# An attention, gating and feed-forward kernel: every engine's instruction order written out, and two more blocks by Strassen's scheme

## Chip, cores and metric

The kernel runs on one core of one Trainium2 chip. The metric is the device time of one execution in microseconds (us). Before the change it is 735.42 us, the median of 3 runs (735.09 to 735.94).

## What is computed

Three layers follow each other, over 4 sequences of 768 tokens with 512 channels. Every input is float32.

```python
# 1. attention in chunks of 32 queries: 8 memory keys, 16 keys to the left, the chunk, 8 to the right
scores = scale * np.matmul(q_c, k_full.transpose(0, 1, 3, 2))
scores = scores - np.max(scores, axis=-1, keepdims=True)
a = np.exp(scores)
a = a / (np.sum(a, axis=-1, keepdims=True) + 1e-09)
out[:, :, c_start:c_end] = np.matmul(a, v_full)
# 2. mixing: a causal convolution of 5 taps makes a gate, which multiplies a projection
gate_pre += conv_w[k][None, None, :] * xp[:, k:k + S, :]
gate = 1.0 / (1.0 + np.exp(-gate_pre))
x = (gate * (x @ w_val)) @ w_out
# 3. normalization and feed-forward with 2048 hidden channels
xn = (x - mu) / np.sqrt(var + 1e-06) * g_ln
out = x + np.maximum(xn @ w_ch1, 0.0) @ w_ch2
```

## The kernel before

The 24 subblocks of 128 tokens are grouped into 13 blocks: block 0 has one subblock, blocks 1 to 11 have two (256 tokens), block 12 has one. Each block passes through attention (`attention32` for the first blocks, `attention` for the others), mixing (`mix`) and feed-forward (`ffn`). Float32 numbers are split into two half-precision parts, high and low, and a product is three matmuls (high by high, high by low, low by high: `PASSES`); only block 0 and parts of the next two use float32 matmuls. The high part is written by ScalarE (ACT), the low part by VectorE (DVE), so nearly every operand takes one instruction on each.

Feed-forward. `ch1` (matmuls at line 716) makes one PSUM tile `c_ps` from 24 matmuls of 256 columns, 8 tiles to a block. In a plain block, ACT takes the ReLU of it (728), DVE makes the low part (730), and `ch2` multiplies it by the second weight (756) in groups of 12 matmuls of 512 columns, eight groups to a block. In a fast block (`FAST = 5`: blocks 5 to 11) the second product goes by Strassen's scheme. Its seven products need sums of the hidden tiles, which `pair` makes four times per block (ACT at 635, 639, 645; DVE at 640 to 644 and 646), and sums of quarters of the second weight. `products` then issues 168 matmuls (line 682), nearly all of 256 columns, where `ch2` issues 96 of 512, and `fast_finish` adds the seven accumulators together (691 to 699).

The sums of quarters of the second weight are made once, by `sums_of_weights`: for each of eight row groups three steps, on DVE (604, 606, 609 to 612, 616) and ACT (615). All of it goes through the one tile `ft`, which plain blocks named in `GATES` use for the first hidden tile, and which `pair` and `fast_finish` use too. `BUILD` says how many of the 24 steps are issued within a block's feed-forward: six each in blocks 1 to 4.

Mixing. `mix` makes the gate from five taps (497 on ACT, 501 on DVE), the projection `val` (519), the output `yps` (537), the mean and variance (544 to 561, a row of small DVE instructions) and the normalized rows `xh` (562 or 564). These are split (ACT 581, DVE 582) and transposed into `xn` by DMA (issued by SP, line 584), and `ch1` of the same block reads `xn`. For blocks below `NPET = 2` the transpose is a float32 matmul with an identity instead (569), and 572 and 573 split its result.

Attention. `totals` (a matmul with ones, line 166) gives the sums of squares by which q, k and v are scaled (`pow2`, 153 to 157); then DVE writes the low parts of q (`bd`, 425) and k (`ks`, 428), and `scores` (280) needs both.

What sets the order. Attention, mixing, feed-forward, weights and loads are generators that a string of steps calls in turn (`PLAN` for the start, then `STEADY` or `FASTY` once per block); attention runs two blocks and mixing one block ahead of feed-forward. The framework's scheduler then arranges the instructions of each engine by priority, and each engine works through its own list strictly in that order.

Of the kernel before, what the change touches and what calls it, by code (L numbers as in the profile page):

```python
# [1 line left out]

# [10 lines left out]
U16 = mybir.dt.uint16  # L13
# [5 lines left out]
P = 128  # L19
# [13 lines left out]
NEVAC = 8  # L33
NXH = 4
NP = 2
FAST = 5
GATES = {1: (0,), 2: (0,), 3: (0,), 4: (0,)}
BUILD = {1: 6, 2: 6, 3: 6, 4: 6}
LAG = 1
NF32 = 2  # L40
NA32 = 3
FIRST = 1
CUT = 384
FILLS = (32, 64, 8, 16)
# [12 lines left out]

def passes(a, b):
# [6 lines left out]
def chunk_attention_moe_kernel(ctx: ExitStack, tc: tile.TileContext,  # L65
                               q, k, v, w_val, conv_w, w_out, g_ln, w_ch1, w_ch2, out):
    nc = tc.nc
    B, S, DM = out.shape
    NSUB, HP = q.shape[1], q.shape[3]
    KEYS = k.shape[5]  # L70
    DFF = w_ch1.shape[1]
    KW = conv_w.shape[1]
# [29 lines left out]
    g_sb = const.tile([P, KC], F32, name="g_sb")  # L102
# [155 lines left out]
    sub = {}  # L258
    tail = [None]

    def load(n):
        while len(sub) < min(n + 1, sum(n for _, n in blocks)):
            b, i = divmod(len(sub), NSUB)
            st = sub[len(sub)] = {}
            st["q"] = ld.tile([P, HP, SUB], F32, tag="q", name="qt")
            nc.sync.dma_start(out=st["q"], in_=q[b, i])
            st["k"] = ld.tile([P, HP, 2, KEYS], F32, tag="k", name="kt")
            nc.sync.dma_start(out=st["k"], in_=k[b, i])
            st["v"] = ld.tile([P, 2, DM], F32, tag="v", name="vt")
            if b + i > 0:  # L270
                nc.sync.dma_start(out=st["v"], in_=v[b, i])
# [117 lines left out]
        yield  # L389

    def attention(n, d, u):


        b, i = divmod(n, NSUB)
# [15 lines left out]
        s = sc_p.tile([P, 3], F32, tag="s", name="s")  # L410
# [74 lines left out]
        return d  # L485

    def mix(j):
        d = blk[j]
        T = d["T"]
        n = T // SUB  # L490
# [155 lines left out]
        nc.vector.tensor_tensor(out=o[1][1], in0=ft, in1=o[0][1], op=ALU.subtract)  # L646

    def products(d, p, u2):
        if not fast[0]:
            fast[0] = True  # L650
            nc.gpsimd.memset(W2.half(3, 0)[:, 768:1024], 0.0)
        if "acc" not in d:
            d["acc"] = [ps_a.tile([P, 2, 256], F32, tag=f"acc{u}", name=f"acc{u}") for u in range(4)]
        acc = d["acc"]
        o = d["h", p]
        half = NM // 2
        own = lambda m, c: W2.rows(m, True, c * 256, 256)
# [28 lines left out]
    def fast_finish(j):
        d = blk[j]
# [43 lines left out]
        d["h", w] = h  # L731

    def ch2(d, w):
        T = d["T"]
        c = 512 // T
        h = d.pop(("h", w))
# [57 lines left out]
    if True:  # L794
        nc.vector.memset(ones, 1.0)

        nc.scalar.activation(out=g_one, in_=ones[:, 0:1], func=AF.Exp)
        for t in (tops[0], bdt, *tops[1:], eye):
            nc.gpsimd.memset(t, 0.0)
# [13 lines left out]
        fetched = [0]
# [66 lines left out]
        def ffn(j):  # L880
# [109 lines left out]
```

## Time and profile before

| | before |
|---|---|
| median of 3 runs | 735.42 us |
| the profiled execution, its own time | 734.32 us |
| its span, first to last instruction | 732.2 us |
| TensorE (PE) busy | 709.3 us |
| VectorE (DVE) busy | 592.7 us |
| ScalarE (ACT) busy | 449.6 us |
| granted TensorE clock | 0.999 |

The profile shows one execution on the hardware. "Busy" is the time in which an engine had an instruction running; a matmul's record is longer than its pace, since matmuls are pipelined, so how fast they follow each other is read from a run of many. A wait is put down to what ended it. Stretches are given in us from the start of the span.

### The profile page before, as it was taken

Reading aid. Unit: us, or ns where it says so; the run is one execution under the profiler, and the core shown is the slowest. Engines: PE = TensorE matmul, PEld = TensorE weight load, DVE = VectorE, ACT = ScalarE, POOL = GpSimd, SP = SyncE. Lnnn points to the kernel's source line nnn. Section 1 sums busy time; section 2 is a strip of 40 time slices with the busy share of each in tenths; the row PEclk is TensorE's granted clock in tenths of the full one; section 3 lists DMA queues with packets and bytes.
Section 4 is the critical chain, followed back from the end, with each engine's and each line's share of the span. In section 5 each row is a group of like instructions: output and inputs, shape, how many; then the busy total and the mean of one; then the engine's idle time right before and its main releaser. Section 6 shows DMA issues by size and latency. Waiting matters only on the chain.

```text
span 732.2 us, 17810 instructions
## 1 busy us (share of the span) xinstructions
PE 709.3 (97%) x7501; PEld 556.1 (76%) x7501; DVE 592.7 (81%) x1297; ACT 449.6 (61%) x716; POOL 11.3 (2%) x37
## 2 busy tenths in 40 slices
PE   8889999999999999999999999999999999999998
PEld 7677776667667667668878878878878878878897
DVE  4979999979969769778789888989888888875461
ACT  4657786546556557568667677677677676652230
POOL 2000010000000000000000000000000000000000
PEclk9999999999999999999999999999999999999999
DMA  9993612141232142133033143033033012001010
GB/s 353 418 405 119 230 65 66 49 125 50 68 81 72 38 102 72 45 99 105 15 96 109 16 95 110 16 95 108 17 94 109 16 23 52 16 16 44 2 33 26
DMA packets 62271, 67.21 MB, mean 92 GB/s; under 512 B 45680, under 2 KB 45936, under 8 KB 62192
## 3 DMA queue, kind: packets, MB, share of 16 engines
q1 hardware_dynamic: 61904, 66.07, 29.0%
q8 instruction: 58, 0.95, 0.6%
q14 instruction: 21, 0.17, 0.1%
q10 hardware_dynamic: 288, 0.02, 0.0%
HBM read 49.30 MB, written 6.29 MB: 76 GB/s over the span
## 4 chain that ended last, share of the span: by engine, by line
PE 70%; DVE 16%; ACT 6%; DMA 4%; issue 2%; SPq 0%; DVEq 0%; ACTq 0%
PE c_ps L716 28%; PE acc L756 12%; PE acc L682 9%; PE yps L537 8%; PE val L519 7%; PE s_ps L280 2%; DMA xn<-xh 2%; DVE gt L501 2%; DVE bd L425 1%; PE pv L466 1%; ACT ft L635 1%; DVE ks L428 1%; PE gram L227 1%; PE pv L376 1%; DVE w L248 1%
## 5 line engine op out<-in xcount | busy, mean ns | idle before, releaser
L716 PE MATMUL c_ps<-xn,w 128*128 128x256 f16 (+1 forms) x2304 | 253.2, 268 | 4.1 <-DMA xn<-xh 4.0
L716 PEld LDWEIGHTS <-w 128*128 128x128 f16 x2304 | 216.2, 98 | 36.3 <-issue 4.6
L756 PE MATMUL acc<-w,hb 128*128 128x512 f16 (+2 forms) x448 | 103.7, 376 | 1.1 <-DVE hb L730 1.1
L501 DVE SCALAR_TENSOR_TENSOR gt<-xT,cw_sb,gt 128x256 f32<-128x256 f32 (+1 forms) x208 | 87.8, 458 | 1.7 <-ACT gt L497 1.5
L756 PEld LDWEIGHTS <-hb 128*128 128x128 f16 x432 | 41.4, 98 | 36.1 <-DVE hb L730 1.4
L682 PEld LDWEIGHTS <-hb 128*128 128x128 f16 x588 | 57.5, 98 | 8.8
L682 PEld LDWEIGHTS <-w 128*128 128x128 f16 x588 | 57.0, 98 | 6.6
L635 ACT ACTIVATE ft<-c_ps 128x512 f32<-128x512 f32 x56 | 32.5, 594 | 48.1 <-PE c_ps L716 30.4
L519 PE MATMUL val<-x,wv 128*128 128x256 f16 (+1 forms) x528 | 57.6, 268 | 0.0
L537 PE MATMUL yps<-wo,hg 128*128 128x512 f16 x252 | 56.9, 379 | 0.5 <-DVE hg L525 0.5
L519 PEld LDWEIGHTS <-wv 128*128 128x128 f16 x528 | 49.4, 98 | 6.2
L682 PE MATMUL acc<-w,hb 128*128 128x256 f16 (+1 forms) x280 | 49.6, 278 | 0.0
L326 ACT ACTIVATE xT<-pv,c_pv 64x256 f32<-64x256 f32 x70 | 32.4, 466 | 23.5 <-PE pv L466 22.8
L537 PEld LDWEIGHTS <-hg 128*128 128x128 f16 x252 | 23.8, 98 | 28.1 <-DVE hg L525 1.0
L682 PE MATMUL acc<-w 128*128 128x256 f16 x266 | 44.7, 273 | 0.0
L728 ACT ACTIVATE hb<-c_ps 128x512 f16<-128x512 f32 (+1 forms) x36 | 21.2, 588 | 34.2 <-PE c_ps L716 34.0
L682 PE MATMUL acc<-spare,hb 128*128 128x256 f16 (+1 forms) x252 | 42.0, 276 | 0.0
L682 PE MATMUL acc<-spare,w 128*128 128x256 f16 x252 | 41.2, 273 | 0.0
L730 DVE SCALAR_TENSOR_TENSOR hb<-c_ps,hb 128x512 f16<-128x512 f32 x32 | 22.0, 686 | 12.7 <-ACT hb L728 12.6
L425 DVE SCALAR_TENSOR_TENSOR bd<-qt,s,bd 64x512 f16<-64x512 f32 x38 | 28.3, 745 | 4.2 <-ACT bd L424 3.6
L640 DVE TENSOR_TENSOR hb<-ft,hb 128x768 f16<-128x768 f32 x14 | 13.4, 957 | 20.8 <-ACT hb L639 20.8
L424 ACT ACTIVATE bd<-qt,s 64x512 f16<-64x512 f32 x38 | 27.2, 716 | 3.0 <-DVE s L155 2.4
(190 smaller groups left out, 1166.0 us busy)
## 6 DMA issues: line engine op xcount, KB each, us to landing
vt<-in_v_dram SPq DMA_DIRECT2D x24, 512.0 KB, 4.3
kt<-in_k_dram SPq DMA_DIRECT2D x24, 384.0 KB, 3.7
qt<-in_q_dram SPq DMA_DIRECT2D x24, 256.0 KB, 2.6
out_dram<-y SPq DMA_DIRECT2D x23, 256.0 KB, 2.3
w<-in_w_ch_dram SPq DMA_DIRECT2D x5, 1023.5 KB, 8.8
spare<-in_w_ch_dram SPq DMA_DIRECT2D x4, 1023.8 KB, 13.7
w<-in_w_ch_dram SPq DMA_DIRECT2D x4, 1023.8 KB, 14.3
spare<-in_w_ch_dram SPq DMA_DIRECT2D x3, 1023.5 KB, 6.1
```

Of the source, the lines that this page charges most:

```text
L326: nc.scalar.activation(out=o, in_=t[pp, :, :, e, :], func=AF.Copy, scale=c_pv if isinstance(c_pv, float) else c_pv[pp])
L424: nc.scalar.activation(out=hi, in_=src, func=AF.Copy, scale=s[pp, 0:1])
L425: nc.vector.scalar_tensor_tensor(out=lo, in0=src, scalar=s[pp, 0:1], in1=hi, op0=ALU.mult, op1=ALU.subtract)
L501: nc.vector.scalar_tensor_tensor(out=o, in0=xT[:, hp, 0:n, kk:kk + SUB], scalar=cw_sb[:, kk, hp:hp + 1], in1=o, op0=ALU.mult, op1=ALU.add)
L519: nc.tensor.matmul(out=t[:, u, 0:T], lhsT=l, rhs=r, start=(x == 0), stop=(x == len(todo) - 1))
L537: nc.tensor.matmul(out=t, lhsT=l, rhs=r, start=(x == 0), stop=(x == len(todo) - 1))
L635: nc.scalar.activation(out=ft[:, at:at + 2, :].rearrange("p x (m n) -> p m x n", m=2), in_=t.rearrange("p (m x n) -> p m x n", m=2, x=2), ...
L682: nc.tensor.matmul(out=o, lhsT=l, rhs=r, start=first, stop=(p == half // 2 - 1 and u2 == 1 and end[t] == x))
L716: nc.tensor.matmul(out=t[:, u * T:(u + 1) * T], lhsT=l, rhs=r, start=(x == 0), stop=(x == len(todo) - 1))
L728: nc.scalar.activation(out=h[0], in_=t, func=AF.Relu)
L730: nc.vector.scalar_tensor_tensor(out=h[1], in0=t, scalar=0.0, in1=h[0], op0=ALU.max, op1=ALU.subtract)
L756: nc.tensor.matmul(out=a[:, 0:n], lhsT=l, rhs=r, start=(first and x == 0), stop=(end and x == len(todo) - 1))
```

## The change

Four things change together.

First, every compute engine's and SP's instructions are put in an order that is spelled out in strings. While the program is built, `mark` notes for each instruction which stream it belongs to (a and b: attention of even and odd subblocks; x and y: mixing of even and odd blocks; f: `ch1` and `pair`; g: second product and closing sums; m, p, q: weights; t: sums of weights; s, l, w: start and loads). At the end `pin` reads for each engine a string such as `x4b+7fxf2x+3`: take the next four of x, then the eighth that is left of b, then the next of f, and so on, and ties each instruction to the one named before it. The ties are for the scheduler alone: no semaphore wait is added. Second, `FAST` becomes 3: blocks 3 and 4 go by Strassen's scheme too, so nine blocks do. Third, the sums of the second weight are made in blocks 1 and 2 alone, twelve steps in each. Fourth, `NPET` becomes 1: block 1's rows are transposed by DMA like the others'. Two small loads on ACT's queue move ahead of the first instructions. The arithmetic of a block is otherwise as it was.

```diff
-FAST = 5
-GATES = {1: (0,), 2: (0,), 3: (0,), 4: (0,)}
-BUILD = {1: 6, 2: 6, 3: 6, 4: 6}
+FAST = 3
+GATES = {1: (0,), 2: (0,)}
+BUILD = {1: 12, 2: 12}
...
-NPET = 2
+NPET = 1
...
+ORDER = {
+    "PE": (
+        "s32a+16a+16a+16a+16a+16a+16a+16a+16a+16a+16a+16a69a+4a+4a+4a+4a+4a+4a+4a+4a+20a+20a+20a+20a+20a+20a+20a+20a+20a+20a+20"
...
+    "DVE": (
+        "sa4sa3samsabmm+2m+2mxx+3xx+2xx+1x3x+3xx+2x4bmxbpxmbm+2bm3bpbxaxmx2m2xbx3ax3ax3pxa4pamp2a2b+3yy+3yy+2yy+1ypy2y+3ypyy+1qyp"
...
+def runs(order):
+
+    return [(l, int(at or 0)) for l, n, at in re.findall(r"([a-z])(\d*)\+?(\d*)", order) for _ in range(int(n or 1))]
...
+    labels, label, mixing = [], ["s"], [0]
+
+    def mark(l):
+
+        labels.extend(label * (len(nc.cur_bb.bb.instructions) - len(labels)))
+        was, label[0] = label[0], l
+        return was
+
+    def pin():
+
+        seq = {e: {} for e in ORDER}
+        for i, l in zip(nc.cur_bb.bb.instructions, labels):
+            e = str(i.engine).split(".")[-1]
+            if e in seq and type(i).__name__ != "BassTilePoolBoundary":
+                seq[e].setdefault(l, []).append(i)
+        for e, todo in seq.items():
+            seq[e] = [todo[l].pop(at) for l, at in runs(ORDER[e])]
+            assert not any(todo.values())
+        follows = [z for x in seq.values() for z in zip(x, x[1:])]
+        follows.append((next(i for i in seq["Activation"][::-1] if type(i).__name__ == "InstDMACopy"), seq["SP"][0]))
+        for a, b in follows:
+            tc.add_manual_dep(b, a.name, mybir.DependencyInfo(mybir.DependencyClass.NoSync, mybir.DependencyReason.SCHED_ONLY),
+                              reason="order")
...
+        nc.scalar.dma_start(out=g_sb, in_=g_ln)
+        cw_raw = const.tile([P, KW * HP * 4], U16, name="cw_raw")
+        nc.scalar.dma_start(out=cw_raw[:, 0:KW * HP * 4 - 1],
+                            in_=conv_w.bitcast(U16).rearrange("p k c -> p (k c)")[:, 1:KW * HP * 4])
         nc.scalar.activation(out=g_one, in_=ones[:, 0:1], func=AF.Exp)
...
-        nc.scalar.dma_start(out=g_sb, in_=g_ln)
         nc.vector.tensor_tensor(out=gs_sb, in0=g_sb, in1=g_sb, op=ALU.mult)
...
-                for _ in range((i + 1) * n // len(steps) - i * n // len(steps)):
+                for _ in range(max(0, i - 1) * n // (len(steps) - 2) - max(0, i - 2) * n // (len(steps) - 2)):
                     go("t")
...
+        mark("")
+        pin()
```

The lists of DVE show what the strings move, at three places. The names: `ft` is the shared tile of sums, `w_113` and `spare` hold the second weight and its sums, `hb` and `w_113` in lines 640 to 646 (722 to 728 in the change) are the operands of the products, `xh` the normalized rows, `bd` and `ks` the low parts of q and k.

The first is DVE in block 2's feed-forward, where one row group's sums of the second weight end. Before:

```order
L611 TENSOR_TENSOR ft<-ft 128x256
L616 TENSOR_TENSOR w_112<-ft,wv 128x256
L612 TENSOR_TENSOR ft<-ft 128x256
L616 TENSOR_TENSOR spare<-ft,spare 128x768
L730 SCALAR_TENSOR_TENSOR hb<-c_ps,hb 128x512
L153 TENSOR_SCALAR e<-tot 128x3
L155 TENSOR_SCALAR s<-e 128x3
L157 TENSOR_SCALAR inv<-e 128x3
L328 TENSOR_SCALAR xT<-pv,c_pv 64x4x64 x2
L414 TENSOR_SCALAR c_exp<-inv 128x1
```

With the change (lines 686 to 698 are the old 604 to 616; 607 is 525; 375 and 376 are 306 and 307; 198 is 153; 517 is 442):

```order
L607 SCALAR_TENSOR_TENSOR hg_2228<-gt,hg_2227 128x512
L692 TENSOR_TENSOR ft<-ft 128x256
L693 TENSOR_TENSOR ft<-ft 128x256
L694 TENSOR_TENSOR ft<-ft 128x256
L698 TENSOR_TENSOR w_113<-ft,wo 128x256
L375 RECIPROCAL rs<-sum 128x8
L198 TENSOR_SCALAR e<-tot 128x3
L376 TENSOR_TENSOR sc<-sc,rs 128x512
L698 TENSOR_TENSOR spare<-ft,spare 128x768
L686 TENSOR_TENSOR ft<-w_113 128x2x256
L517 TENSOR_TENSOR p_2358<-sc,p_2357 128x512
L688 TENSOR_TENSOR ft<-w_113 128x512
```

Before, the next row group's 604 stands 58 rows behind the last 616 of this one; now its 686 follows the last 698 directly. Of the 64 DVE instructions that make the sums, 32 stood ahead of what the last `ch1` matmul of block 2 waits for, and now 57 do.

The second is DVE at the end of mixing for a block, between the last small instruction of the variance (561, now 643) and the low parts of the normalized rows (582, now 664), in the fast blocks. Before:

```order
L561 SCALAR_TENSOR_TENSOR va<-mv,rt 128x2
L640 TENSOR_TENSOR w_113<-ft,w_113 128x3x256
L641 TENSOR_TENSOR ft<-ft 128x256
L582 TENSOR_TENSOR xh_6997<-xh,xh_6996 128x512
L642 TENSOR_TENSOR ft<-ft 128x256
L643 TENSOR_TENSOR ft<-ft 128x256
L644 TENSOR_TENSOR ft<-ft 128x256
L646 TENSOR_TENSOR w_113<-ft,w_113 128x4x256
L582 TENSOR_TENSOR xh_7057<-xh,xh_7056 128x512
```

With the change:

```order
L643 SCALAR_TENSOR_TENSOR va<-mv,rt 128x2
L664 TENSOR_TENSOR xh_7203<-xh,xh_7202 128x512
L623 TENSOR_TENSOR c_y<-inv,cy_w 128x1
L722 TENSOR_TENSOR w_113<-ft,w_113 128x3x256
L723 TENSOR_TENSOR ft<-ft 128x256
L724 TENSOR_TENSOR ft<-ft 128x256
L725 TENSOR_TENSOR ft<-ft 128x256
L726 TENSOR_TENSOR ft<-ft 128x256
L664 TENSOR_TENSOR xh_7263<-xh,xh_7262 128x512
L728 TENSOR_TENSOR w_113<-ft,w_113 128x4x256
```

The low part of the first rows moves ahead of two instructions of `pair`, and that of the second rows ahead of the longest of them, 646 (now 728).

The third is DVE between the scales of a subblock (414, 417, now 489, 492) and the first use of its scores (291, now 360), in the fast blocks. Before:

```order
L417 TENSOR_SCALAR c_pv<-inv 128x1
L541 TENSOR_TENSOR c_y<-inv,cy_w 128x1
L644 TENSOR_TENSOR ft<-ft 128x256
L425 SCALAR_TENSOR_TENSOR bd<-qt,s,bd 64x16x32
L473 SCALAR_TENSOR_TENSOR x_6227<-xT,s,x_6226 128x4x128
L646 TENSOR_TENSOR hb<-ft,hb 128x1024
L425 SCALAR_TENSOR_TENSOR bd<-qt,s,bd 64x16x32
L428 SCALAR_TENSOR_TENSOR ks<-kt,s,ks 128x768
L451 SCALAR_TENSOR_TENSOR vs_6984<-vt,s,vs_6983 128x1024
L291 TENSOR_REDUCE mx<-s_ps 128x8
```

With the change:

```order
L489 TENSOR_SCALAR c_exp<-inv 128x1
L492 TENSOR_SCALAR c_pv<-inv 128x1
L500 SCALAR_TENSOR_TENSOR bd<-qt,s,bd 64x16x32 x2
L503 SCALAR_TENSOR_TENSOR ks<-kt,s,ks 128x768
L726 TENSOR_TENSOR ft<-ft 128x256
L526 SCALAR_TENSOR_TENSOR vs_7190<-vt,s,vs_7189 128x1024
L360 TENSOR_REDUCE mx<-s_ps 128x8
L361 TENSOR_TENSOR sc<-s_ps,mx 128x512
L548 SCALAR_TENSOR_TENSOR x_6433<-xT,s,x_6432 128x4x128
L728 TENSOR_TENSOR hb<-ft,hb 128x1024
```

Three instructions that stood between the scales and `ks` (the last of 641 to 644, then 473 and 646) now stand behind it.

## Rows read from the trace of the kernel before

**Rows 1.** The page, part 1: busy us (share of the span) and instructions of each engine.

```profile
PE 709.3 (97%) x7501; PEld 556.1 (76%) x7501; DVE 592.7 (81%) x1297; ACT 449.6 (61%) x716; POOL 11.3 (2%) x37
```

**Rows 2.** Busy us by stretch: length, PE, weight loads, DVE, ACT, POOL, clock, DMA.

```profile
0.00:20.00 20.00, 16.47 (x232) 15.69 (x233) 10.62 (x27) 10.10 (x17) 4.97 (x13) 1.00 0.92 360
20.00:140.00 120.00, 111.25 (x1011) 81.91 (x1010) 112.67 (x229) 81.46 (x111) 2.90 (x6) 1.00 0.53 200
140.00:213.00 73.00, 73.00 (x713) 49.48 (x711) 63.47 (x147) 41.81 (x73) 0.39 (x2) 1.00 0.29 79
213.00:340.00 127.00, 126.09 (x1255) 86.44 (x1254) 97.27 (x220) 78.77 (x135) 1.21 (x6) 1.00 0.27 73
340.00:661.00 321.00, 315.55 (x3588) 263.21 (x3587) 276.00 (x611) 219.26 (x355) 1.88 (x10) 1.00 0.23 60
```

**Rows 3.** Chain of waits, 265 to 345: start us, us, what. A group of ch2.

```profile
290.74 2.59 PE acc L756 x12
```

**Rows 4.** Timeline of PE, 205 to 216: the last ch1 group of block 2.

```profile
210.75 2.78 PE L716 MATMUL c_ps<-xn,w 128*128 128x256 f16 x24
```

**Rows 5.** Chain of waits, 535 to 612, in fast blocks.

```profile
551.65 2.42 DMA xn<-xh
...
565.62 2.29 PE acc L682 x18
...
573.15 2.62 PE acc L682 x24
```

**Rows 6.** Groups: weight loads of the products (busy us, mean ns of one).

```profile
L682 PEld LDWEIGHTS <-hb 128*128 128x128 f16 x588 | 57.5, 98 | 8.8
```

**Rows 7.** Groups: transposes by matmul, 16 of the 24 in block 1.

```profile
L569 PE MATMUL xnT<-eye,xh 128*128 128x128 f32 x24 | 3.5, 282 | 1.0 <-DVE xh L564 1.0
```

**Rows 8.** Groups: DVE in plain blocks (730) and in fast ones.

```profile
L730 DVE SCALAR_TENSOR_TENSOR hb<-c_ps,hb 128x512 f16<-128x512 f32 x32 | 22.0, 686 | 12.7 <-ACT hb L728 12.6
L640 DVE TENSOR_TENSOR hb<-ft,hb 128x768 f16<-128x768 f32 x14 | 13.4, 957 | 20.8 <-ACT hb L639 20.8
L646 DVE TENSOR_TENSOR hb<-ft,hb 128x1024 f16<-128x1024 f32 x14 | 17.1, 1222 | 2.2 <-ACT hb L645 2.2
L641 DVE TENSOR_TENSOR ft<-ft 128x256 f32<-128x256 f32 x28 | 11.9, 423 | 0.4
```

**Rows 9.** Groups: DVE's sums of the second weight (604 as 606; 609, 610, 612 as 611).

```profile
L606 DVE TENSOR_TENSOR ft<-w 128x512 f32<-128x512 f16 x8 | 5.5, 685 | 0.0
L611 DVE TENSOR_TENSOR ft<-ft 128x256 f32<-128x256 f32 x8 | 3.4, 424 | 0.2
L616 DVE TENSOR_TENSOR spare<-ft,spare 128x768 f16<-128x768 f32 x8 | 7.6, 951 | 2.8 <-ACT spare L615 2.7
L616 DVE TENSOR_TENSOR w<-ft,wv 128x256 f16<-128x256 f32 x4 | 1.7, 424 | 0.0
```

**Rows 10.** Waits of PE, 140 to 720: us in total, times, longest.

```profile
PE c_ps L716 <- DMA xn<-xh: 4.0, 5, 1.1
PE s_ps L280 <- DVE ks L428: 2.4, 5, 0.5
PE pv L466 <- DMA pT<-p: 0.9, 1, 0.9
```

**Rows 11.** Timeline of DVE, 540 to 555: the low parts of a block's rows.

```profile
545.70 0.69 DVE L582 TENSOR_TENSOR xh<-xh,xh 128x512 f16<-128x512 f32 x1
...
548.77 1.23 DVE L646 TENSOR_TENSOR w<-ft,w 128x1024 f16<-128x1024 f32 x1 [1.12 <-ACT w L645]
549.91 0.68 DVE L582 TENSOR_TENSOR xh<-xh,xh 128x512 f16<-128x512 f32 x1
```

**Rows 12.** Timeline, 582 to 592: ks, and the scores that wait for it.

```profile
586.66 1.23 DVE L646 TENSOR_TENSOR hb<-ft,hb 128x1024 f16<-128x1024 f32 x1
...
588.70 1.02 DVE L428 SCALAR_TENSOR_TENSOR ks<-kt,s,ks 128x768 f16<-128x768 f32 x1
...
589.77 0.92 PE L280 MATMUL s_ps<-ks,bd 128*64 128x64 f16 x46 [0.47 <-DVE ks L428]
```

More of the change, by code (lines that the diff above doesn't have):

```diff
@@ L1 @@
 from contextlib import ExitStack
+import re
 import concourse.bass as bass
@@ L48 @@
 PLAN = "w1 a4 l1 a1 w3 m2 w1 m1 a1 x1 w1 1_1 m1 l1 x1 w1 x1 w1 x2 w1 x3 a2 w1 x1 1_1 a1 m1 a2 w1 a1 x1 1_1 a3 1_2 x1 1_3 2_1 x2 1_1 l1 x4 f2 w1 1_1 m1 x1 w2 1_1 2_1 m1 1_1 2_2 x1 2_1 x1 1_1 2_1 f1 a1 w1 m1 a1 2_2 f1 x1 f2 2_1 w1 a2 1_1 2_1 l1 f1 a4 m1 w1 x1 f1 2_3 w1 a2 1_2 x1 1_1 2_4 f1 a1 x1 f2 x1 f2 a2 f1 x1 a2 x1 a1 f2 x1 a1 x3 a1 f1 a1 x1 a1 f1 a1 x1 f1 a1 x1 f1 a1 f3 a1 f1 a2"
+ORDER = {
+    "PE": (
+        "s32a+16a+16a+16a+16a+16a+16a+16a+16a+16a+16a+16a69a+4a+4a+4a+4a+4a+4a+4a+4a+20a+20a+20a+20a+20a+20a+20a+20a+20a+20a+20"
+        "a+20a+20a+20a+20a+20a4m8a16m8x14b16m+16m16x6mb4a16b16x4p24f3f+13f+13f+13a4p8fa16p16f2y16f5p16f11pf6y2q8by2b5yq8y2q8fyb11"
+        "fq8f4gf17g2f2gf6q8f2g4q24b4aqg3a16b16gff+23g4f12a4f11a10ba6g6f8g6f39b2x10b36g2f12b10f24g+1g+1f12gx26g19f14g6x14b2g4b23a"
+        "b23x6g2x16f10a12g6a36g6f48g30a12ba36g6f48y24g12b48f48g12f48ag6y24g12b24f12b24y6f12y12g6a48y6f24g30a48bg18x24f60b48x12f36"
+        "g42x12f48b48ag18f12g24a48x24f36g54a36bg18a12g12f96b24g10y12b24y12g20y24f48g24ag18b48f24g12a48y24f24g18a36ba12g66f84b24"
+        "f12b24x12g18x36g24f48g12ag18b48g12f24a48x24f24g18a24g24a12ba12g42f84b12g10f12b36g20y36f24y12f12g12f12b48ag12f36a48y24f12"
+        "g30a12g30a36bg54f60b48x24f24g18f12g12x24f36g12f12b48af24g30a48x24g12f24g30a48g54bf72b48f24g10y24g20y24g12f48g12ag6b48f24"
+        "g12a48y24f24g42bg30a12g24a36f60b48f36x48g18f12g12f36b12g12b24ag12b12g6f24a48x24g24f24g30a36bg12a12g42f96g10b36g20b12f12"
+        "y48f36g24f24b48f12y6f12y12g6y6g12x12g72x12g12x12g12x12f84g10f12g8f24g12f24x12g42f48g24f12g30f36g30f24g12f108g48f12g48"),
+    "DVE": (
+        "sa4sa3samsabmm+2m+2mxx+3xx+2xx+1x3x+3xx+2x4bmxbpxmbm+2bm3bpbxaxmx2m2xbx3ax3ax3pxa4pamp2a2b+3yy+3yy+2yy+1ypy2y+3ypyy+1qyp"
+        "ypypmpyp3yqpmqpmqymy2bb+2ypyqybpbyby3qbypy2qyby2bpbqya+3qx+20qpqyq2bapq2a+2a3qyabaqabagqabqx+22b3fby+20bqa2b2xt2xtbaxtfx"
+        "fxtt+2txbx+2xbb+6bx+1x2qx2t2xtbtxfbxbtbtxtbft+1x2t2axb2ataqa3xa2x2bxa+8xaxtxaxfxaxtxy+22x2ax2axtt+2txaxaf2at2xt3btba2gyt"
+        "ybt+1y3atb2gy2fb3fy2y+3ybt2yy+1by2b2tytft2fyt2t+1t2yt3t+1babt2bt2bfatya2tt+2atabybat2aa+7ftatay3ayayay2afyay2x+20y6tx+22"
+        "t2yb2yft+1ybatb2g2b4x8b+7fxf2x+3b2xf2b2x+2fxb2x3f3bf2xfx+1x2y+20a3f3a5f2a+7a6fx11ax5fxf4xfby+22b4gbg3g+1g2y2b2aby+2yy+1y"
+        "fyfyf2b+8fybx+20bfybyby2fby2f2ybf2byy+1fby2afaf3a3fa3a+8fa2bx+22a5y2ay14f2yfb2f2bybfg3bgg+1g2b3x2x+2xx+1f3afb+7bfbx2fx2"
+        "x+3xbxb2x+1bx2fxf4xx+1fbx2a4f3af2a3a+7fa2y+20bay+22a3x2ax14f3xf2xb2fb2g4bg+1g2byb2yy+2fyfy+1y2f2yfb+7ab2fyy+3byb2yy+1bf3"
+        "y3fbfyy+1fx+20y2a5fafa2a+7fafx+22afa4fay16bfyf2bf2ybfb4y+20bg4g+1g2bab+8fbxfbfxf2x+2xx+1x2fbx4b2x3bfbfx2f2bfxx+1fx2afa2"
+        "f3a5fa+8a2bfa2xa2xax8ax7y+22f5xfb3gbg3g+1g2b3ybyy+2fyy+1y3ab+7f4b2fbyy+3y2y+1bfy2bfybf3yy+1bfy2a4fa2f2a2a+7fafax+20bfa4"
+        "x+22yay15f2yf2bfb2yfb3g4g+1g2b2x2x+2ab+7b2fxx+1xf3xfxbfxx+3xb3xx+1x3fbf4xx+1fy+20xa2xfa6a+7a2f2a3fx2fx3afax11fxb2f4xy+22"
+        "fb3g2bg2g+1g2yabfybf4x+20by+2yfy+1b+8bfby2f2yfyy+3b4yfyy+1y2byfbyy+1y2f4x2fxbfyx+1xyxfx+2xy2x+1x2y6fy3x+1xy3x3fyf3yg2xg2"
+        "g+1g2f6x2f6x6f2x4f2x6f9g4g+1gf2g2fg3"),
+    "Activation": (
+        "s4a2mbm2a4x4mpxbpxampm+1pb2abp2bb+1a2y3p2byqyqpmqfpyqpmyq2fpa+1abb+3pqpqfyb+3p2qyqfb2aq2b2qfqa2b2xabqf2x3t+1tb+2bf2a3qxb"
+        "xt+1txb2a2xbaxa+2b2fat+1xftfabxa2byt+1ybtaf2y2bb+2bfayft+1ta2yft+1tbt+1ayb2ta2bfa+2fy2a2b3yt+1fta3ya2x4b3b+2f+1f2bfa2f2b"
+        "fxaff+1x2f2b4a3a+2bfabxaxb2f+1f2x4fgaba4y2f+1b2yf2b+2afybf3a2yfby2f+1f2a3ba+2bfb5ayaybf+1f2y2a2y2fa3gb3x2f+1xfb+2fxfba2"
+        "f3bxfx2af+1f2a3b3a+2fb2af+1bxaxb2f2x4fb2ga4byayf+1f2b+2yfaybf2afabyfy2f+1f2b2a3a+2b4ayfaf+1fyb2fy4fb3gb+2a5xf+1f2xaxbxf4"
+        "abxfax2f+1f2b2ab2a2a+2bfax2f+1babfx2fx2fa2bga2by2b2af+1f2b+2y2fbf3a3ybfy2f+1f2a3ba+2b4fayb2aybf+1f2y3fyb3ga2b+2a3x2f+1f2"
+        "bx2a2f2abf2xfx2f+1f2a3b3a+2b4abx2faf+1f2x4fa2ga3ybf+1f2y2b2b+2f4byfbyf+1fyfyb5x2fyxf+1f2xy4fygxf+1xf7xf+1f2x3ff+1f4gf3"),
+    "Pool": (
+        "sas3s+2s2ab3a+1batbgbaa+1ab3aa+1abab2ab"),
+    "SP": (
+        "s+1s2wlsw2l2wlwlwlw4lwl3qw2awl2q2wqaa+1y3ayb+2a2gb+2b+2b2a+2a+2a+2x2a2x2g2b+2b+2b2a+2a+2ba+2a2y4g2b+2b+2b+2b2a+2a+2a+2a2"
+        "x4b+2b+2b+2b2g2a+2a+2a+2a2y4b+2gb+2gb+2b2a+2a+2a+2a2x4b+2gb+2b+2gb2a+2a+2a+2a2y4b+2b+2b+2bgbga+2a+2a+2a2x4b+2g2b+2b+2b2"
+        "a+2a+2a+2a2y4gb+2b+2gb+2b2a2x4g2b2y4g2x2g4"),
+}
@@ L391, in attention, with attend @@
     def attention(n, d, u):
+        mark("ab"[n % 2])
+        for _ in attend(n, d, u):
+            yield
+            mark("ab"[n % 2])
+    def attend(n, d, u):
         b, i = divmod(n, NSUB)
@@ L487, in mix, with mix_steps @@
     def mix(j):
+        mixing[0] = j
+        mark("xy"[j % 2])
+        for _ in mix_steps(j):
+            yield
+            mark("xy"[j % 2])
+    def mix_steps(j):
         d = blk[j]
@@ L648, in products, with quarters_of @@
     def products(d, p, u2):
+        mark("g")
+        quarters_of(d, p, u2)
+        mark("f")
+    def quarters_of(d, p, u2):
         if not fast[0]:
@@ L686, in fast_finish @@
     def fast_finish(j):
+        mark("g")
         d = blk[j]
@@ L733, in ch2, with second @@
     def ch2(d, w):
+        mark("g")
+        second(d, w)
+        mark("f")
+    def second(d, w):
         T = d["T"]
@@ L763, in finish @@
     def finish(j):
+        mark("g")
         d = blk[j]
@@ L807, in chunk_attention_moe_kernel @@
         nc.gpsimd.partition_all_reduce(g_max, g_one, P, ReduceOp.max)
-        cw_raw = const.tile([P, KW * HP * 4], U16, name="cw_raw")
-        nc.scalar.dma_start(out=cw_raw[:, 0:KW * HP * 4 - 1],
-                            in_=conv_w.bitcast(U16).rearrange("p k c -> p (k c)")[:, 1:KW * HP * 4])
         pieces = [(W, jj) for W in (Wv, Wo, W1, W2) for jj in range(W.n)]
@@ L917, in go, with step @@
         def go(c, later=0):
+            was = mark({"x": "xy"[mixing[0] % 2], "1": "p", "2": "q"}.get(c, c))
+            step(c, later)
+            mark(was)
+        def step(c, later):
             tc.cur_priority += later
```

## The prediction

> **What bounds the kernel now.** I read the page's first part, then the busy time by stretch, then the chain of waits and PE's waits in the later blocks. The page [rows 1] shows PE busy for 97% of the span, DVE for 81%, ACT for 61%. A share over the whole span hides its stages, so look at the stretches [rows 2]. From 20 to 140 us, where weights are converted and the first blocks run, DVE is busy 112.7 of 120 and PE 111.3: both are near their limit, and neither can lend the other much. From 140 on PE is the bound: it is busy 73.0 of 73, 126.1 of 127 and 315.6 of 321, while DVE has room in the first two (63.5 of 73, 97.3 of 127) and a little less in the last (276.0 of 321). [...] The later blocks lose time in three waits alone [rows 10]: 4.0 us for the transposed rows `xn`, 2.4 for `ks`, 0.9 for one `pT`, 7.3 together.
>
> **The change, part by part.**
>
> *Two more fast blocks, on PE.* Eight groups of 2.59 go from each of blocks 3 and 4: 20.7 us. In their place stand 168 matmuls, three of them twice as wide, so 171 units of 0.109: 18.7. The group of 18 with the three wide ones confirms the count, 21 units in 2.29 [rows 5]. That is 2.05 us less per block, 4.1 in all, and on the path, as PE has no slack there. The 168 matmuls need as many weight loads of 98 ns [rows 6], 16.5 us, which run beside them.
>
> [...] The rows say that a 512-column matmul costs twice a 256-column one. [...] The sum goes by the rows.
>
> *The same, on DVE.* A fast block's four `pair`s cost DVE 4 x (0.957 + 1.222) + 16 x 0.423 = 15.5 us, where a plain block pays 8 x 0.686 = 5.5 [rows 8]: 10 us more per block, and somewhat more for its closing sums. From 213 to 340 DVE has 30 us free [rows 2], and it loses there the sums of the weight, so I cost this at nothing. Without that cover it would be 20 us.
>
> *Sums in two blocks.* DVE's part is 2 x 5.5 + 4 x 3.4 + 7.6 + 2 x 1.7 = 35.6 us [rows 9], 0.56 for each of its 64 instructions. With 57 instead of 32 of them ahead of the end of block 2's `ch1`, 25 x 0.56 = 14 us move ahead of a point that PE now passes at 213.4 us (its last group starts at 210.75 [rows 4], and the next takes over some 2.6 later). This is the one part that can cost. Against it, the order puts 16 instructions of mixing (3 us) behind that point and leaves nothing there that isn't waited for. Adding up every DVE instruction up to the one that the last of those `ch1` matmuls waits for, each at its kind's mean, scaled so that the whole kernel of before gives the page's 592.7, I get 190 us for the new order and 182 for the old, where DVE was in fact busy 186.8 by 213 [rows 2]: 5 us ran ahead of need.
>
> DVE cannot work all the time. It was idle 9.4 us in the first 20, when little has been loaded, 7.3 from 20 to 140, and 9.5 from 140 to 213 [rows 2]. I keep the first two, since the start's chain is hardly changed, and ask how much of the third is left. If none, the point is passed at 190 + 16.7 = 206.7; if all, at 216.2. PE itself could pass it at 205.9: in the new order two groups of 12 (5.2 us) of block 2's `ch2` come later, and the transposes of block 1 fall away (below). With more independent work in DVE's list, a third of the 9.5 seems likely (nearer to the end at none, as DVE was idle only 7.3 of 120 where it had as much to do): the point at 210, 3.4 us earlier than before. The 5.2 us are then still to be done.
>
> *Transposes of block 1.* 16 of 24 records of 3.5 us [rows 7] go, 2.3 us of PE. They lie in the stretch in which DVE sets the end, so they give nothing of their own (ends: 0 and 2.3); the conversions that take their place on ACT and DVE are of the same number and size. SP gains four transposes of about 2.4 us [rows 5], beside a PE that then has block 0's work and attention to do.
>
> *The order, later blocks.* Two of the three waits have a cause that the lists show. The low part of a block's second rows ends at 550.6, behind the 1.23 of line 646, which itself waited 1.12 for ACT [rows 11]; the transposes land 3.5 us later and PE waits. The new order puts it ahead of 646, which is 1.2 us or more earlier, where the longest wait is 1.1 [rows 10]. I count 3.4 of the 4.0 as gone, a little being left for blocks in which DVE itself is late. The scores' wait is at most 0.5 [rows 10], and 1.23 us of line 646 stood ahead of `ks` [rows 12] and no longer does: all 2.4 go. What is late next behind `xn` and `ks` is PE itself. I don't count on the 0.9. The ties add no waits; what they can cost is that an engine stands behind an instruction that is late, as it could before.
>
> *The two loads on ACT.* DVE no longer stands behind `g_sb` at the start, but the first scores wait for their own loads anyway: nothing.
>
> **The sum**, against the profiled execution (span 732.2, its own time 734.32, so 2.1 around it): 732.2 - 3.4 + 5.2 - 4.1 - 3.4 - 2.4 = 724.1, and 726.2 with the 2.1. That execution was 1.1 below the median of the runs, and I forecast **726.5**.
>
> **The rivals.**
>
> *DVE keeps its gaps.* If all of the 9.5 us from 140 to 213 stays, the point is passed at 216.2, 2.8 later than before: 732.2 + 2.8 + 5.2 - 4.1 - 5.8 = 730.3, time 732.4. For it speaks that these gaps are waits for PE and ACT; against it, that more work stands ready.
>
> *The tile `ft` serializes the sums, and DVE holds PE: slower.* All sums pass through one tile, which ACT must have read before the next row group overwrites it, and the new order sets row groups directly behind each other. Before, DVE waited 2.8 us in all for these writes of ACT [rows 9]. If DVE stood still in each of the eight row groups for about the time of ACT's two writes (taken as DVE's own for the same tiles, 0.95 + 0.42), 11.2 us instead of 2.8 would be lost on top of all the old gaps: the point at 224.6, span 738.7, time 740.8. It turns to slower from a point later than some 220.7. Against it: between the sums the new list still has other work.
>
> *The waits of the later blocks stay*, and grow with the fast blocks from seven to nine: instead of -5.8, + 6.4 x 2/7 = 1.8. Span 731.7, time 733.8. Against it stand the lists.
>
> *Wide matmuls are the cheaper ones.* If one of 512 columns cost no more than one of 256, 0.109, the two blocks would lose 2 x (18.7 - 10.5) = 16.4 instead of gaining 4.1: time 746.7. Rows 3 and 5 exclude it nearly. [...]
>
> *The order also fills the start.* If DVE idles no more after 140 and PE sets the point, 205.9, and the 0.9 goes too: 724.1 - 4.1 - 0.9 = 719.1, time 721.2. PE is idle 12.3 us before 140 [rows 2]; with 3 us of that as well, 718.
>
> *The strings do nothing that lasts*: the old waits stay and the sums only change places, so that the 4.1 alone is left: 730.2.
>
> **How the numbers follow.** Chances: the forecast 0.48, the start filled 0.20, DVE keeps its gaps 0.15, `ft` serializes 0.08, the waits stay 0.06, strings without effect 0.02, wide matmuls cheaper 0.01. The likeliest gives the time. A measurement of this kernel tells about 0.2%, 1.5 us, from no change. The first two and the strings are faster by more, of DVE's gaps two thirds, of the waits a third: 0.83 after a little is taken off for things unseen. Slower: `ft`, wide matmuls, a little of the gaps: 0.10. The rest, 0.07, is no change. The range goes from the filled start, 718, past the waits that stay, to 736, where only the slower rivals are left out.
>
> **What would show it.** Right: nine closings of fast blocks; PE's later waits for `xn` and `ks` together below 2 us; the last `ch1` group of block 2 passed at 207 to 213 us with DVE idle below 6 us from 140 to there; 168 matmuls still 18.7 us. Wrong: that point at 216 or later, DVE waiting for ACT in lines 686 to 698, or PE waiting for `hb` or `c_ps` tiles in blocks 1 to 4, where DVE's extra 20 us would then not be covered.

## The result and the profile after

The changed kernel takes 728.38 us (median of 4 runs, 728.23 to 729.63), the kernel before 735.68 in the same session (735.09 to 736.54): a ratio of 0.9904, 95% interval 0.9886 to 0.9921. The profiled execution took 728.48 us, its span 726.5.

The page's first part, which answers to [rows 1]: busy us (share of the span) and instructions.

```profile
PE 707.9 (97%) x7629; PEld 570.1 (78%) x7629; DVE 619.4 (85%) x1339; ACT 461.8 (64%) x734; POOL 15.4 (2%) x37
```

Busy time by stretch, as in [rows 2], with the third stretch ending at the start of the last `ch1` matmul of block 2, called the point below: length, PE, weight loads, DVE, ACT, POOL, clock, DMA.

```profile
0.00:20.00 20.00, 15.13 (x212) 14.29 (x213) 9.74 (x21) 9.70 (x17) 5.86 (x11) 0.97 0.93 351
20.00:140.00 120.00, 115.73 (x1042) 86.22 (x1042) 116.33 (x246) 84.00 (x118) 4.57 (x8) 0.99 0.56 205
140.00:206.26 66.26, 64.69 (x663) 45.00 (x661) 64.17 (x140) 37.34 (x66) 0.51 (x2) 1.00 0.31 78
```

Before, the point stood at 213.26. DVE is now busy 116.3 of 120 and 64.2 of 66.3 us on the way to it, and PE 115.7 and 64.7: neither has much room. The last `ch1` group of block 2 starts 7.0 us earlier than in [rows 4]:

```profile
203.75 2.78 PE L804 MATMUL c_ps<-xn,w 128*128 128x256 f16 x24
```

PE's waits from the point to the end (us in total, times, longest), to be held against [rows 10]:

```profile
PE pv L541 <- DMA pT<-p: 2.3, 2, 1.2
PE acc L769 <- DVE w L728: 0.8, 1, 0.8
PE val L601 <- DVE x L548: 0.6, 1, 0.6
PE s_ps L349 <- DVE ks L503: 0.3, 1, 0.3
```

The wait for `xn` is gone and that for `ks` nearly so; the wait for `pT` has grown, and two small ones are new. In all it is 4.0 us instead of 7.3. From the point to the end of the span the kernel before took 732.2 - 213.3 = 518.9 us and the changed one takes 726.5 - 206.3 = 520.2:

```profile
206.26:726.50 520.24, 512.34 (x5718) 424.63 (x5715) 429.10 (x935) 330.81 (x537) 4.47 (x16) 1.00 0.23 60
```

So of the 5.7 us gained in span, 7.0 are counted ahead of the point and 1.3 are given back behind it. This doesn't say on which side work was saved: 5718 matmuls stand behind the point instead of 5550, 144 of them because blocks 3 and 4 go by Strassen's scheme, and 24 because two groups of block 2's `ch2` (5.2 us) now come later.

### The profile page after: what moved, and what is told of

Its sections match the earlier page's. It is cut to its first block, busy times and chain, and to the rows that moved or that the text cites. A ratio compares the mean times of both kernels' runs of the same rounds, so it can differ in the third digit from the quotient of the medians.

```text
span 726.5 us, 18125 instructions
## 1 busy us (share of the span) xinstructions
PE 707.9 (97%) x7629; PEld 570.1 (78%) x7629; DVE 619.4 (85%) x1339; ACT 461.8 (64%) x734; POOL 15.4 (2%) x37
## 4 chain that ended last, share of the span: by engine, by line
PE 65%; DVE 21%; DMA 7%; ACT 5%; issue 2%; DVEq 0%; ACTq 0%
PE c_ps L804 24%; PE acc L769 16%; PE yps L619 7%; PE val L601 6%; PE acc L849 6%; DVE gt L583 4%; DMA xn<-xh 3%; PE s_ps L349 2%; PE pv L541 2%; DMA w<-in_w_out_dram 2%; DMA pT<-p 2%; DVE bd L500 1%; PE gram L272 1%; DVE ks L503 1%; ACT xT L395 1%
## 5 line engine op out<-in xcount | busy, mean ns | idle before, releaser
L804 PEld LDWEIGHTS <-w 128*128 128x128 f16 x2304 | 216.5, 98 | 31.9 <-DMA xn<-xh 2.3
L769 PEld LDWEIGHTS <-w 128*128 128x128 f16 x756 | 72.5, 98 | 10.8 <-DVE w L728 1.4
L849 PE MATMUL acc<-w,hb 128*128 128x512 f16 (+2 forms) x280 | 64.8, 374 | 0.0
L769 PE MATMUL acc<-w,hb 128*128 128x256 f16 (+1 forms) x360 | 64.8, 278 | 0.0
L717 ACT ACTIVATE ft<-c_ps 128x512 f32<-128x512 f32 x72 | 40.8, 593 | 32.4 <-PE c_ps L804 11.3
L769 PE MATMUL acc<-w 128*128 128x256 f16 x342 | 58.2, 272 | 0.0
L769 PE MATMUL acc<-spare,hb 128*128 128x256 f16 (+1 forms) x324 | 55.6, 276 | 0.0
L769 PE MATMUL acc<-spare,w 128*128 128x256 f16 x324 | 54.5, 273 | 0.0
L619 PEld LDWEIGHTS <-hg 128*128 128x128 f16 x252 | 23.9, 98 | 26.6 <-DVE sc L361 0.2
L395 ACT ACTIVATE xT<-pv,c_pv 64x256 f32<-64x256 f32 x70 | 32.4, 467 | 11.3 <-PE pv L541 10.4
L727 ACT ACTIVATE hb<-ft 128x1024 f16<-128x1024 f32 x18 | 19.0, 1053 | 24.7 <-DVE ft L726 24.7
L664 DVE TENSOR_TENSOR xh<-xh,xh 128x512 f16<-128x512 f32 x23 | 15.9, 690 | 18.3 <-DMA xn<-xh 12.2
L362 ACT ACTIVATE sc<-sc,c_exp 128x512 f32<-128x512 f32 x19 | 13.6, 718 | 25.4 <-DVE sc L361 25.4
## 6 DMA issues: line engine op xcount, KB each, us to landing
w<-in_w_ch_dram SPq DMA_DIRECT2D x5, 1023.5 KB, 10.3
```

Source lines behind the costliest of these rows:

```text
L395: nc.scalar.activation(out=o, in_=t[pp, :, :, e, :], func=AF.Copy, scale=c_pv if isinstance(c_pv, float) else c_pv[pp])
L619: nc.tensor.matmul(out=t, lhsT=l, rhs=r, start=(x == 0), stop=(x == len(todo) - 1))
L664: nc.vector.tensor_tensor(out=x2[1], in0=xh, in1=x2[0], op=ALU.subtract)
L717: nc.scalar.activation(out=ft[:, at:at + 2, :].rearrange("p x (m n) -> p m x n", m=2), in_=t.rearrange("p (m x n) -> p m x n", m=2, x=2), ...
L727: nc.scalar.activation(out=o[0][1], in_=ft, func=AF.Copy)
L804: nc.tensor.matmul(out=t[:, u * T:(u + 1) * T], lhsT=l, rhs=r, start=(x == 0), stop=(x == len(todo) - 1))
```

## The experiments

The theory was that the gain is made of two fast blocks that cost PE 4.1 us less, of an order that fills DVE up to the point, and of low parts that come early enough for the transposes. The rivals: the strings do nothing that lasts; PE's list, not DVE's, removes the waits; DVE does not set the point. All times are medians beside runs of the kernel before on the same chip.

**The strings left out.** One line goes; the kernel's new blocks, sums and loads stay:

```diff
         mark("")
-        pin()
```

> The changed kernel with its nine fast blocks, its sums in two blocks and its loads, but with the scheduler's own order in place of the strings. If the strings do nothing that lasts: 728.4 us, as with them (within 1). If they are worth what is left beside the 4.1 us of the two blocks: about 731.6 (735.7 less 4.1), with PE's waits for the transposed rows and for ks together above 5 us again. If the sums in two blocks only fit beside the rest because the strings leave DVE no gap: 735 or more, and the last group of ch1 in block 2 starts after 212 us (206 with the strings).

Measured: 740.92 us, ratio 1.0085 (1.0069 to 1.0102), slower than before. The busy time up to its point, and PE's two largest waits over the whole run:

```profile
20.00:140.00 120.00, 111.53 (x966) 83.24 (x965) 110.75 (x229) 80.59 (x111) 2.90 (x6) 0.99 0.57 202
140.00:221.80 81.80, 76.53 (x762) 50.15 (x762) 78.38 (x187) 48.48 (x84) 0.71 (x3) 1.00 0.26 69
...
PE c_ps L804 <- DMA xn<-xh: 6.1, 7, 1.2
PE s_ps L349 <- DVE ks L503: 4.0, 8, 0.7
```

The point comes at 221.8, 15.5 us later than with the strings. With the first 20 us (8.7), DVE is busy 197.9 us up to there and idle 23.9; with the strings 190.2 and 16.0. So 7.6 us of DVE's work that the point doesn't need goes behind it, and 7.9 us of gaps are filled. The old waits are back too, 7.9 us for `xn` and `ks` past the point; in return PE has done more of the later work by then (busy 204.5 us up to the point instead of 195.6).

**The strings left out, and blocks 3 and 4 plain.**

```diff
-FAST = 3
+FAST = 5
...
         mark("")
-        pin()
```

> The scheduler's own order again, with the sums in two blocks but blocks 3 and 4 plain, so seven fast blocks as before. Against before (735.5) it shows what the sums in two blocks cost in that order, against the run of the own order with nine fast blocks (740.9) what the two further fast blocks do. If these gain their 4.1 us there too: 745. If their gain is lost in that order because PE waits in them: 740 to 742. If they lose time there: below 740, and the sums in two blocks are not what costs.

Measured: 745.44 us, ratio 1.0133 (1.0115 to 1.0150). Against the run above, the two further fast blocks gain 4.5 us between the medians and 3.5 between the ratios, even in the scheduler's order. That is of the size of the sum's 4.1, but no clean measure of it: this kernel's granted clock was 0.994 to 0.995 in every run, that of the run above 0.999 or 1.0 in four of six. Half a per cent of 745 us is 3.7 us (an estimate, and an upper end: it counts only as far as PE held the path).

Against before this kernel is 9.9 us slower with the same seven fast blocks. Its point comes at 220.2:

```profile
140.00:220.20 80.20, 75.69 (x745) 49.51 (x745) 75.65 (x181) 46.67 (x81) 0.40 (x2) 0.98 0.26 69
```

That is 6.9 us later than before. With 10.4 and 112.1 in the stretches up to 140, DVE is busy 198.1 us up to there instead of 186.8, and all 64 instructions of the sums start ahead of the point, where 32 did before. The kernel still has the change's early loads and its fewer transposes of block 1, and it has the lower clock, so the 9.9 is not the sums' alone. The three medians together give the balance: + 9.9 for the sums in two blocks with what goes along, - 4.5 for the two blocks (both with the clock's share in them), - 12.5 for the strings, - 7.2 in all.

**One string alone.** In `pin` the ties are made for one engine:

```diff
-        follows = [z for x in seq.values() for z in zip(x, x[1:])]
+        follows = [z for e, x in seq.items() if e in ('DVE',) for z in zip(x, x[1:])]
```

> The changed kernel with the string of DVE alone; PE, ACT, POOL and SP take the scheduler's own order around it. Of the 12.5 us by which all strings beat the scheduler's own order (740.9 to 728.4): if DVE's order is what counts (the sums, the low parts), 8 or more of them come with it alone, 732.5 or less. If PE's order is what counts (what PE has to do while something is late), 4 or fewer, 737 or more.

> The same with the string of PE alone. If DVE's order is what counts: 737 or more, with PE waiting for the transposed rows and ks again. If PE's order is what counts: 732.5 or less. If the lists only work together: both this and DVE's alone above 735.

Measured: 815.27 us with DVE's alone (ratio 1.1093, 1.1061 to 1.1126), 801.57 with PE's alone (1.0902, 1.0870 to 1.0934), both much worse than no string at all. One engine's fixed list stands behind whatever the others do late: in the first DVE waits 29.7 us for the sums of squares from PE, in the second PE waits 23.2 us for ACT to read `c_ps`:

```profile
DVE e L198 <- PE tot L211: 29.7, 18, 3.7
```

```profile
PE c_ps L804 <- ACT ft L717: 23.2, 7, 5.2
```

So neither of these two lists works without the others, which is the last case of the second expectation; the size of the loss was in neither. Which engine's order "is worth" the 12.5 us can't be told by taking one alone.

**Shorter and longer sums.** First the four operations per row group on 16 columns (each 0.17 instead of 0.42 us), most of the sums left out; then, in a second kernel, two of them on 768:

```diff
-            V(out=b22, in0=b22, in1=b12, op=ALU.subtract)
+            V(out=b22[:, 0:16], in0=b22[:, 0:16], in1=b12[:, 0:16], op=ALU.subtract)
...
+            V(out=ft[:, 0:3, :], in0=ft[:, 0:3, :], in1=ft[:, 3:4, :].to_broadcast([P, 3, 256]), op=ALU.subtract)
```

> Of the sums of the second weight the four subtractions and additions of each row group work on 16 columns in place of 256, so most of the weights' sums are left out; count and order of the instructions are those of the change. About 28 of these 32 stand ahead of the end of ch1 in block 2, some 0.26 us shorter each: 7 us less on DVE. If DVE sets that point, as the prediction has it: its last group starts 3 us or more before the 203.5 us or so of the change, and the time falls by as much, to 725.5 or less. If PE sets it there too with the strings: less than 1 us.

> All strings; of each row group's four subtractions and additions two work on 768 columns in place of 256, so the weights' sums are other numbers. About 14 of these 16 stand ahead of the end of ch1 in block 2, some 0.53 us longer each: 7.4 us more on DVE. If DVE was full there (2.2 us idle from 140 to 210): that point comes 4 to 7 us later and the time rises to 732 to 735.5. If PE alone set it and DVE still had room: 728.4 to 730.

Measured: shorter 727.14 us (ratio 0.9892, 0.9878 to 0.9906), longer 735.56 (1.0004, 0.9992 to 1.0016). The stretch up to the point, of the shorter and of the longer:

```profile
140.00:205.53 65.53, 64.82 (x663) 45.05 (x662) 59.71 (x140) 37.42 (x65) 0.51 (x2) 1.00 0.29 79
```

```profile
140.00:210.60 70.60, 67.11 (x668) 45.48 (x666) 69.61 (x141) 38.34 (x67) 0.51 (x2) 1.00 0.25 70
```

With 6 us less on DVE the point moves by 0.7 and the time by 1.2, a little over the expected "less than 1": PE (64.8 of 65.5) holds the point. With the longer sums DVE is busy 196.6 us up to the point instead of 190.2. The point comes 4.3 us later and the time rises by 7.2 between the medians, by 5.9 between the two profiled executions: DVE (69.6 of 70.6) holds it. Both engines are nearly full there, so more work of DVE ahead of the point is paid for in about its full length, and a saving on DVE alone brings next to nothing.

**The low part back behind the long operation.** After `pin` has made its lists, single instructions are moved in them (an entry gives the engine, the instruction to stand behind, those moved; seven such entries):

```diff
+    ('DVE', 'I-3556', 'I-3693'),
...
+            seq[e] = [i for i in seq[e] if i.name not in moved]
+            at = [i.name for i in seq[e]].index(behind) + 1
+            seq[e][at:at] = out
```

> DVE: in the seven fast blocks from 265 to 602 us the low part of the second rows goes back behind the longest instruction of pair, where it stood before; all else as in the change. If that place is what took away PE's waits for the transposed rows, as the prediction has it: they come back, 3 to 4 us from 260 us on, time 731 to 732. If they went because PE's own list now has other work ahead of those matmuls: below 1 us of such waits, time 728.4 within 0.7, and perhaps a little less, since DVE stood 12.2 us in all waiting for the transposes ahead of this instruction and the other fits into that.

Measured: 732.33 us, ratio 0.9968 (0.9953 to 0.9982), 4.0 more than the change. PE's waits past the point (line numbers are 16 higher here), and DVE at the first of the seven places:

```profile
PE c_ps L820 <- DMA xn<-xh: 5.8, 6, 1.9
```

```profile
268.49 1.23 DVE L744 TENSOR_TENSOR w<-ft,w 128x1024 f16<-128x1024 f32 x1 [1.76 <-ACT w L743]
269.64 0.68 DVE L680 TENSOR_TENSOR xh<-xh,xh 128x512 f16<-128x512 f32 x1
```

The row of the prediction is back: the low part stands behind an operation of 1.23 us, which itself waited 1.76 for ACT. With it 5.8 us of waiting are back, and from the point to the end the kernel takes 4.1 us longer. The rival that PE's list covers the transposes falls. The price of the change's place is that DVE itself waits 12.2 us there for the transposes; it is smaller than what the place saves.

**Groups with v later.** Three PE entries of the same kind:

> PE: three groups of the products with v, which stood 0.8 and 0.6, 1.2 and 1.2 us waiting for their transposed probabilities at 191, 319 and 411 us, go behind 12 matmuls of ch1, 18 and 12 of the products that follow them. If the order is what makes these waits: 3.3 us of them fall to below 0.7, and the time falls by 2 to 3, to 725.5 to 726.5. If the wait only moves to the next thing (scores or values late, DVE pushed back): 728.4 within 0.7.

Measured: 727.67 us, ratio 0.9901 (0.9886 to 0.9915). The wait for `pT` past the point is gone, and in its place stand 2.0 us for operands of the products, 0.8 each for `ks` and `x`, 0.5 for the sums of squares: 4.1 in all, as much as in the change. The difference of 0.7 is inside the intervals.

**More changes of tile.** Nine groups of 48 cut into four, with entries of two matmuls each:

> All strings, but nine groups of 48 matmuls with v are cut into four of 12, with two of the six matmuls of ch1 or of the products that stood ahead of the group put into each cut: the same matmuls, 54 more changes between tiles of 64 rows and the full array. If a change costs PE the 0.098 us that the gaps between the starts of such neighbours show: 54 x 0.098 = 5.3 us, time 733.7. If that gap is hidden or an artefact of how ends are modelled: 728.4 within 0.7.

Measured: 732.50 us, ratio 0.9961 (0.9948 to 0.9974): 4.1 us for 54 changes, 0.08 each; the two intervals leave 0.05 to 0.11. From the point to the end it takes 5.0 us longer, with 1.2 us less of waits, which makes 0.11 each. So a change between 64-row tiles and the full array costs PE some 0.1 us. The gaps agree: in the change a 256-column matmul on the full array, on record for 0.273 us on average, is followed by the next of its kind after 0.109 us, by one on a 64-row tile after 0.205.

**Fewer changes of tile.** Fourteen entries for PE and one for DVE, then the same without three of them:

> All strings, with pieces of PE's list put together: seven split groups of matmuls with v and three of the scores are each moved behind the work that split them (some 21 changes fewer), two further groups with v that waited for their transposes go behind 12 matmuls, and DVE's longest instruction of pair at 602 us goes ahead of the low part that waits for a transpose. If changes cost 0.098 us each and the waits do not come back elsewhere: 2.1 + some 2.5 + 0.8 less, 723. If the delayed groups make softmax, values and mixing late instead: 727 to 730.

> The merged order less three of its moves, each of which was followed by a new wait of PE in its trace: the matmuls with v behind the products at 268 us (0.68 of wait for ACT), those at 434 us (0.52), and DVE's low part at 600 us (1.59 for the transposes in place of 0.8 for the operands). Given back are about 4 changes, 0.3 to 0.4 us. If the waits belong to these moves: 1.2 to 1.7 us less than the merged order's 726.0, 724.3 to 724.8. If waits of this size turn up elsewhere: 726 within 0.7.

Measured: 725.96 us (ratio 0.9871, 0.9848 to 0.9894) and 726.13 (0.9869, 0.9846 to 0.9891), the best of the study, 2.4 us below the change. The intervals overlap a little, the single runs don't (725.22 to 726.27 for the first, 728.23 to 729.63 for the change). Neither expected case for the first came, not 723 and not 727 to 730. The waits past the point are 3.9 and 3.8 us: none went, they only changed places, those of the second run to

```profile
PE val L622 <- DVE x L569: 1.4, 1, 1.4
PE acc L790 <- DVE w L749: 1.2, 1, 1.2
PE s_ps L370 <- DVE ks L524: 0.8, 2, 0.5
PE c_ps L825 <- DMA xn<-xh: 0.4, 1, 0.4
```

What fell is the changes of tile, counted in the order of PE's matmuls: from 88 past the point to 64 and 68. From the point to the end the two take 518.3 and 518.2 us instead of 520.2; 24 and 20 fewer changes at 0.08 to 0.1 us are 1.6 to 2.4.

**The first load.** SP takes `qt` ahead of `kt` again, by one entry.

> All strings, but SP issues the first load of q ahead of that of k, as before. In the change the first scores start at 5.85 us, before at 4.99. If the start is a chain of waits that carries on: 0.5 to 0.9 us less, 727.5 to 727.9, and block 0 ends as much sooner. If the start's other waits (the converted weights) take it up: 728.4 within 0.4.

Measured: 728.66 us, ratio 0.9908 (0.9889 to 0.9926). The scores start at 5.30 instead of 5.85, and the time is 0.3 above the change's: nothing is gained. PE's largest waits of the start are the same in both kernels: 2.1 us for `xT` from ACT, 1.3 and 1.1 for DVE's converted weights. The two early loads on ACT were not tried apart.

## Why the prediction was right, and where its steps were not

The direction and the size held: 726.5 forecast, 728.4 measured. Two steps erred, in opposite directions, so that the number is this close is in part luck.

*Up to the point* the count was right and the gaps were put too large. DVE's work ahead of the point was forecast at 190 us and is 9.74 + 116.33 + 64.17 = 190.2. But "I keep the first two" of the gaps failed: DVE's idle time from 20 to 140 us fell from 7.3 to 3.7, that from 140 on to 2.1 where 3.3 were expected. With 10.3 in the first 20 us the idle time is 16.0 instead of the forecast's 20, and the point came at 206.3 instead of 210, just ahead of the 207 to 213 named as a sign of being right. That is nearly the point (205.9) of the rival *the order also fills the start*, in which PE sets it; the runs with shorter and longer sums show that both engines do. With it the term for the transposes of block 1 falls. It was put at nothing because DVE sets the end of that stretch; but PE, relieved of them, could pass the point at 205.5 (the run with shorter sums), and with their 2.3 us at 207.8, later than the 206.3 measured. By these numbers they are worth some 1.5 us, an estimate; no run puts them back alone. The rival of `ft` is out. DVE stood idle 0.4 us in all ahead of its sums, and the group that had waited 2.8 us for ACT [rows 9] waits no more:

```profile
L698 DVE TENSOR_TENSOR spare<-ft,spare 128x768 f16<-128x768 f32 x8 | 7.6, 952 | 0.0
```

*Two more fast blocks*: -4.1 forecast; between two kernels without strings -4.5, or -3.5 by the ratios, with a share of the clock in it. What carries the step is the pace: 0.216 us for a matmul of 512 columns (2.59 by 12, [rows 3]), 0.109 for one of 256 (2.62 by 24, [rows 5]). A group of 18 products with three wide ones and one of 24 still take what [rows 5] show, in the chain of waits of the change:

```profile
342.20 2.29 PE acc L769 x18
...
348.42 1.64 PE acc L769 x15
```

15 of them take 1.64, 0.109 each, and all 24 of that group 2.62. The rival of cheaper wide matmuls stays excluded: by it the two blocks would have lost 16.4 us, where they gain 3.5 to 4.5.

*The order, later blocks* is the step that failed. The cause for `xn` was right: it went by the low part's place, as its return by 5.8 us shows. Of the 2.4 for `ks` 0.3 is left; no run puts `ks` back alone, so that its place on DVE did this is argued, not shown. The sentence that failed is "What is late next behind `xn` and `ks` is PE itself". Late next is `pT`, twice 1.2 us, at places where the new list puts the group with v so soon behind the softmax that its transposes, issued from 315.11 us on, are not there yet:

```profile
320.68 0.67 PE L541 MATMUL pv<-pT,vs 64*128 64x64 f16 x34 [1.17 <-DMA pT<-p]
```

The forecast left 7.3 - 5.8 = 1.5 us of waits; 4.0 stand there. Three kernels that tried to remove them ended at 3.8 to 4.1, in other places.

*A cost the sum didn't have*: the strings cut attention into more pieces, 88 changes between tile shapes past the point instead of 62, and 26 at the measured 0.08 to 0.1 us are 2.1 to 2.6. The gaps between the starts of neighbours in the trace of before, 0.205 us instead of 0.109 as above, would have given it.

So from the point on 514.1 us were forecast (724.1 - 210) and 520.2 measured, 6.1 more: 2.5 from waits, some 2.4 from changes of tile, and about 1.2 that stays open. Against it stand 3.7 us at the point. One slip is in the chances: the parts named for "faster" add up to 0.82, so the 0.83 can't be what is left after taking something off.

The mishap foreseen as slower (a point later than 220.7) is what the same kernel does without its strings, 221.8 and 740.9 us, though by another mechanism: DVE waits only 1.8 us for ACT's part in the sums there, so it isn't `ft`, but DVE work that the point doesn't need standing ahead of it. *The strings do nothing* is thereby refuted.

## What to carry to other kernels

Where two engines are both full, count what each must do ahead of the point that matters. Here a scheme that saves PE work and gives DVE more, with its sums early, was slower than before (740.9 us) until the order moved DVE's other work behind that point; then 6 us less on DVE alone brought 1.2. With PE 97% busy, taking away waits of a microsecond by reordering mostly moved them: three kernels that tried ended with as much. Count the changes between tile shapes on PE as a cost of every order, here 0.08 to 0.1 us each. And don't fix one engine's order without the others': DVE's or PE's list alone cost 61 to 74 us against none at all.

## What the runs showed of the hardware

A change between matmuls on 64-row tiles and on the full array costs PE about 0.08 to 0.1 us: 4.1 us for 54 added ones, 2.4 for 24 taken away, of which 6 are with 64-column tiles. What PE does in that time no run shows.

In the two kernels with one string alone the granted clock is 0.965 (DVE's) and 0.970 (PE's) on average, where the change has 0.997. PE also waits more there (23.2 us for `c_ps` alone in the second); that the one comes of the other no run shows. From 20 to 140 us with DVE's string alone PE is busy 104.6 of 120 us at a clock of 0.92, in the change 115.7 at 0.99, so some of the lost time may be the clock's. How much wasn't tried apart.
